# Other chunk sizes in the first mixture, and the second transform's pieces tied to their places on TensorE

## The chip, the cores and the metric

The kernel runs on one core of one Trainium2 chip. The metric is the device time of one execution in microseconds (us), the median over several runs. TensorE (PE in the profile) does the matrix products, VectorE (DVE), ScalarE (ACT) and GpSimd (POOL) the elementwise work. SyncE (SP) issues the transfers between the core's memory and the chip's main memory, in order, from one queue.

## The reference

The input is x, 2 batches of 3136 rows of 256 numbers. Three layers follow each other.

```
Y  = rfft(x, axis=1) mixed by complex weights w_r, w_i, plus bias; soft threshold 0.01
x1 = irfft(Y, n=3136)                                       # layer 1: Fourier filter
x2 = x1 + relu(layernorm(x1) * g @ w1) @ w2                 # layer 2: MLP 1, 256 -> 1024 -> 256
u  = x2 + real(fft(fft(x2, axis=1), axis=2))                # layer 3: a 2-D transform,
out = u + relu(layernorm(u) @ v1) @ v2                      #          then MLP 2
```

Every row passes both MLPs by itself; the transforms along axis 1 join all 3136 rows of a batch. So MLP 2 of a batch needs all of that batch's x2, and batch 1 of a stage can run beside batch 0 of the next.

## The kernel before

**Stages.** Layer 1 runs in three stages (forward transform, mixing, inverse). Its results go to main memory as `dY`, one array per batch. MLP 1 reads rows of `dY` and stores x2 to `dX`. The transform along the rows is split into a 49-point and a 64-point part. The class `Stage98` does the first of these: 16 steps for each batch (`s4[0]`, `s4[1]`), which read 98 x 512 pieces `r` of `dX` (line 352), split them on POOL and ACT (lines 371 to 373 and 204), multiply (line 222 and the two after, into the buffers `psc`), and store the result `o` to `dA` (line 427). `middle` (line 384) gathers one column of `dX` ahead of them. The class `Front` does the rest for each pair of rows of MLP 2: it loads from `dA` (line 764), does four small products (`stage_b`, line 780), and then the transform over the 256 channels (`dmix`, lines 805 to 817), whose sum is the input of MLP 2.

**MLPs.** Both MLPs run in chunks of up to 4 tiles of 128 rows. A chunk has a first layer `l1` with 8 parts f, each 6 matmuls at lines 222 to 224 into one of three buffers `psa`. Each part is evicted twice: by ACT (line 697, relu) and then by DVE (line 699, the remainder `l`, so that two numbers of fewer bits stand for one). A second layer `l2` follows, one tile at a time, each 16 matmuls at lines 715 and 716 into one of two buffers `psb`, evicted by DVE (719, 720) and stored by SP (728). Batch boundaries do not fall on chunks: one tile takes 64 rows from each batch (the shared tile).

**Input of a chunk.** While a chunk runs, the input of the next is made: statistics (DVE 608, 609), `norm` (ACT 616, 630, 631; DVE 617 to 620), `flip` (DVE 643, a transpose of 32 x 32 blocks, then a store of `dT` by SP at 649), `land` (SP 656 reads it back as `q`), and `split` into high and low part (ACT 204, DVE 212). Only then can its `l1` start.

**What sets the order.** A scheduler with a simulated timeline orders the instructions of each engine; `issue_after(x)` adds an edge that holds an instruction behind instruction x on the same engine and makes no semaphore. `run_mlp` gives the places: tables such as `USUAL`, `LATE`, `FIRST`, `EARLY` say at which part (`("l1", f)` or `("l2", tile)`) of a chunk the next one's pieces are written, and `hook` puts the steps of `Stage98` at the places of `STAGE4_AT` (MLP 1, batch 0) and `STAGE4_MLP2` (MLP 2, batch 1). SP works its queue in that order, and a transfer that reads what an earlier one wrote waits there for it.

In `chunks1` MLP 1 has 13 chunks: for batch 0 of 4, 4, 4, 4, 2, 4 and 3 tiles (the last with the shared tile), for batch 1 six of 4. MLP 2 has 13 chunks as well. I write c0 to c12 and m0 to m12 for them.

## Time and profile before

| | |
|---|---|
| median of 3 runs (lowest to highest) | 822.72 us (822.21 to 823.26) |
| profiled execution | 821.94 us |
| its span, first to last instruction | 820.0 us |
| PE busy in the span | 789.9 us (96%) |
| DVE, ACT, POOL busy | 543.0, 363.3, 124.2 us |
| mean granted TensorE clock | 0.994 of full speed |

The profile follows one execution. Each row of a timeline names the engine, the line of the code, the operation, what it writes and reads, and in brackets how long the engine stood idle before it and which engine or transfer ended the idle time. PE is busy nearly all the time, so the places where it is not, about 30 us in the whole span with the start and the end, are where the order of the work can matter.

### The profile page before, as it was taken

The numbers are of one execution on the slowest core, as the hardware profiler recorded it, in microseconds if no ns is written. First come the engines' busy times: TensorE is split into PE (matmuls) and PEld (weight loads), VectorE is DVE, ScalarE is ACT, GpSimd is POOL, SyncE is SP. The second block draws the span as 40 slices with busy tenths as digits, with TensorE's granted clock in tenths as the row PEclk, the third lists the DMA queues.
The fourth block names the chain that finished last, engine by engine and source line by source line (L and its number), as shares of the span: only waits on it lengthen the run. The fifth ranks groups of instructions, "written<-read, shape, count | busy, mean of one in ns | idle before, by whom it ended". The sixth has DMA issues, their size and how long they took to land.

```text
span 820.0 us, 12035 instructions
## 1 busy us (share of the span) xinstructions
PE 789.9 (96%) x4276; PEld 656.4 (80%) x4276; DVE 543.0 (66%) x1260; ACT 363.3 (44%) x791; POOL 124.2 (15%) x152
## 2 busy tenths in 40 slices
PE   8999999999997999999999998999989999999996
PEld 3888977967676879887788886888768898888885
DVE  6479996478846687666747884557555667676543
ACT  1422356358744643345332544456443545444321
POOL 1222221220000000055400002465220000000000
PEclk9999999999999999999999999999999999999999
DMA  8742200621445333454653224454543343322211
GB/s 229 216 137 86 78 1 2 213 103 36 157 145 176 129 110 106 119 172 154 189 157 107 70 74 129 144 155 141 158 116 113 101 138 120 88 71 72 63 36 32
DMA packets 79663, 95.16 MB, mean 116 GB/s; under 512 B 16610, under 2 KB 58858, under 8 KB 79408
## 3 DMA queue, kind: packets, MB, share of 16 engines
q1 hardware_dynamic: 79604, 94.40, 37.9%
q8 instruction: 34, 0.56, 0.3%
q14 instruction: 25, 0.20, 0.1%
HBM read 56.89 MB, written 37.49 MB: 115 GB/s over the span
## 4 chain that ended last, share of the span: by engine, by line
PE 64%; DMA 12%; DVE 11%; SPq 4%; ACT 4%; issue 2%; POOL 1%; DVEq 0%; ACTq 0%; POOLq 0%
PE psb L715 17%; PE psb L716 9%; PE psa L222 8%; PE psa L223 8%; PE psa L224 8%; PE psb L482 4%; DMA yb<-dY 3%; PE psc L780 2%; SPq L328 2%; PE psc L303 2%; PE psa L450 2%; DVE st L608 2%; PE psc L322 2%; PE psc L502 2%; DMA dA<-o 1%
## 5 line engine op out<-in xcount | busy, mean ns | idle before, releaser
L697 ACT ACTIVATE h<-psa 128x512 fp32r<-128x512 f32 (+2 forms) x208 | 116.5, 573 | 219.3 <-PE psa L224 164.8
L699 DVE SCALAR_TENSOR_TENSOR h<-psa,h 128x512 fp32r<-128x512 f32 (+2 forms) x208 | 134.0, 653 | 70.8 <-ACT h L697 68.8
L715 PE MATMUL psb<-r2b,h 128*128 128x512 f32 x392 | 138.2, 399 | 0.0
L715 PE MATMUL psb<-r3a,h 128*128 128x512 f32 x392 | 136.6, 397 | 0.0
L716 PE MATMUL psb<-r2b,h 128*128 128x256 f32 x392 | 106.4, 282 | 0.0
L716 PE MATMUL psb<-r3a,h 128*128 128x256 f32 x392 | 105.4, 282 | 0.0
L222 PE MATMUL psa<-u0r,r3a 128*128 128x512 f32 (+2 forms) x208 | 83.6, 403 | 7.3 <-DVE h L699 7.2
L482 PE MATMUL psb<-wm,h 128*128 128x256 f32 (+1 forms) x600 | 88.8, 298 | 0.8 <-DVE w L488 0.8
L715 PEld LDWEIGHTS psb<-r2b,h 128*128 128x128 f32 x392 | 72.0, 188 | 14.7
L715 PEld LDWEIGHTS psb<-r3a,h 128*128 128x128 f32 x392 | 71.4, 188 | 15.3 <-PE psa L224 0.5
L222 PE MATMUL psa<-u0r,r2b 128*128 128x512 f32 (+2 forms) x208 | 81.7, 393 | 1.9 <-DVE w L207 1.7
L482 PEld LDWEIGHTS psb<-wm,h 128*128 128x128 f32 (+1 forms) x600 | 76.1, 189 | 8.7 <-issue 8.1
L223 PE MATMUL psa<-u0r,r2b 128*128 128x512 f32 (+2 forms) x208 | 79.3, 381 | 0.0
L224 PE MATMUL psa<-u0r,r2b 128*128 128x512 f32 (+2 forms) x208 | 79.2, 381 | 0.0
L223 PE MATMUL psa<-u0r,r3a 128*128 128x512 f32 (+2 forms) x208 | 78.7, 379 | 0.0
L716 PEld LDWEIGHTS psb<-r3a,h 128*128 128x128 f32 x392 | 73.8, 189 | 4.0 <-issue 0.5
L716 PEld LDWEIGHTS psb<-r2b,h 128*128 128x128 f32 x392 | 74.1, 189 | 3.1
L224 PE MATMUL psa<-u0r,r3a 128*128 128x512 f32 (+2 forms) x208 | 75.8, 380 | 0.1
L719 DVE TENSOR_TENSOR o<-psb,yb 128x256 f32<-128x256 f32 x76 | 31.4, 421 | 60.7 <-PE psb L716 60.0
L204 ACT ACTIVATE yg<-psc 98x512 f32<-98x512 f32 (+2 forms) x58 | 48.5, 859 | 45.4 <-PE psc L502 26.9
L222 PEld LDWEIGHTS psa<-u0r,r3a 128*128 128x128 f32 x208 | 39.1, 188 | 20.0 <-DVE h L699 12.4
L212 POOL TENSOR_TENSOR h<-w 128x512 f32<-128x512 f32 (+1 forms) x26 | 34.5, 1328 | 109.2 <-DVE w L489 70.3
(119 smaller groups left out, 1272.7 us busy)
## 6 DMA issues: line engine op xcount, KB each, us to landing
dT<-q SPq DMA_DIRECT2D x20, 512.0 KB
q<-dT SPq DMA_DIRECT2D x20, 512.0 KB
s<-in_moe_w_ch_dram SPq DMA_DIRECT2D x16, 512.0 KB
r<-dX SPq DMA_DIRECT2D x32, 196.0 KB
dA<-o SPq DMA_DIRECT2D x32, 196.0 KB
dY<-yg SPq DMA_DIRECT2D x12, 512.0 KB
r<-dA SPq DMA_DIRECT2D x48, 128.0 KB
dX<-o SPq DMA_DIRECT2D x11, 512.0 KB
```

What stands on the lines that cost most here:

```text
L204: nc.scalar.activation(out=o, in_=i, func=AF.Copy, scale=scale)
L212: ins = eng.tensor_tensor(out=o, in0=a, in1=b, op=ALU.subtract)
L222: nc.tensor.matmul(out=ps, lhsT=lh, rhs=rh, start=first, stop=False)
L223: nc.tensor.matmul(out=ps, lhsT=ll, rhs=rh, start=False, stop=False)
L224: ins = nc.tensor.matmul(out=ps, lhsT=lh, rhs=rl, start=False, stop=last)
L303: nc.tensor.matmul(out=ps, lhsT=cam, rhs=self.raw[g // 2][:, e * 512:(e + 1) * 512], start=True, stop=True)
L482: nc.tensor.matmul(out=ps[0:m, u * D:(u + 1) * D], lhsT=xv[:, o:o + m], rhs=wm_hl[wv][:, e, c, :], start=k == 0, stop=k == 11)
L697: ins = nc.scalar.activation(out=h[:, 0:n], in_=ps[:, 0:n], func=AF.Relu)
L699: ins = nc.vector.scalar_tensor_tensor(out=l[:, 0:n], in0=ps[:, 0:n], scalar=0.0, in1=h[:, 0:n], op0=ALU.max, op1=ALU.subtract)
L715: nc.tensor.matmul(out=ps, lhsT=h[:, ts_], rhs=w2[:, f, :], start=f == 0, stop=False)
L716: nc.tensor.matmul(out=ps[:, 0:D], lhsT=l[:, ts_], rhs=w2[:, f, 0:D], start=False, stop=f == NF - 1)
L719: nc.vector.tensor_tensor(out=o, in0=ps[:, 0:D], in1=self.y[:, i, :], op=ALU.add)
```

## The change

The first mixture's chunks become 4, 4, 4, 4, 4, 4 tiles for batch 0 and 3 (with the shared tile), 3, 4, 4, 4, 4 and 3 for batch 1: still 13 chunks and 49 tiles. The seventh chunk, c6, takes its statistics at new places (`SIXTH`). The 16 steps of `Stage98` go to 6, 6 and 4 places in three chunks, in place of 6, 5 and 5, so that the last step stands at the first tile of the third chunk's `l2` and not at its last. Every step, and `stage_b` of MLP 2's input, is held on PE behind the last matmul written for the chunk at that place (`self.pe`). `ahead` loads a third piece before the second split, so each load is issued one group earlier. The arithmetic and the number of matmuls are the same. The changed kernel's lines stand 3 to 7 further down: 699 is now 704, 608 is 612, 780 is 787.

```diff
@@ -32,16 +32,19 @@
 FIRST = {"stats": (("l2", 0),) * 4, "norm": ("l2", 3), "flip": (("n", 0), ("n", 1))}
 EARLY = {"stats": (("l1", 0), ("l1", 0), ("l1", 1), ("l1", 1)), "norm": ("l1", 2), "flip": (("l1", 5), ("l1", 6)),
          "land": ("l2", 2)}
+SIXTH = {"stats": (("l1", 5), ("l1", 5), ("l1", 6), ("l1", 6)), "norm": ("l1", 7), "flip": (("l2", 1), ("l2", 2))}
 USUAL = {"b": (1, 3), "mix": (3, 5), "stats": (("l1", 4), ("l1", 6)), "norm": ("l1", 7), "flip": (("l2", 1), ("l2", 2))}
 LATE = {"b": (4, 6), "mix": (6, 7), "stats": (("l1", 7), ("l2", 0)), "norm": ("l2", 0), "flip": (("l2", 2), ("l2", 3))}
 LAND_AT = ("l1", 3)
 PREP0_AT = (23, 24)
 L2_BEHIND = 7
 APPLY_POOL = (0, 1)
-STAGE4_AT = ((8, "l1", 6), (8, "l1", 7), (8, "l2", 0), (8, "l2", 1), (8, "l2", 2), (8, "l2", 3)) + tuple(
-    (k, *at) for k in (9, 10) for at in (("l1", 2), ("l1", 5), ("l2", 0), ("l2", 1), ("l2", 3)))
-STAGE4_MLP2 = ((1, "l1", 1), (1, "l1", 3), (1, "l1", 5), (1, "l2", 0), (1, "l2", 1), (1, "l2", 3)) + tuple(
-    (k, *at) for k in (2, 3) for at in (("l1", 2), ("l1", 5), ("l2", 0), ("l2", 1), ("l2", 3)))
+STAGE4_AT = ((8, "l1", 6), (8, "l1", 7)) + tuple((8, "l2", i) for i in range(4)) + tuple(
+    (9, *at) for at in (("l1", 1), ("l1", 3), ("l1", 5), ("l2", 0), ("l2", 1), ("l2", 3))) + tuple(
+    (10, *at) for at in (("l1", 1), ("l1", 3), ("l1", 5), ("l2", 0)))
+STAGE4_MLP2 = tuple(
+    (k, *at) for k in (1, 2) for at in (("l1", 1), ("l1", 3), ("l1", 5), ("l2", 0), ("l2", 1), ("l2", 3))) + tuple(
+    (3, *at) for at in (("l1", 1), ("l1", 3), ("l1", 5), ("l2", 0)))
 STAGE4_FROM = ((7, "l2", 0), (0, "l2", 0))
 WARM_UP = 10
 TB = 2
@@ -400,6 +403,7 @@
 
         def ahead(self):
             self.split()
+            self.load()
             self.split()
 
         def step(self):
@@ -692,6 +696,7 @@
                     c == 0, c == 1)
             if f == L2_BEHIND:
                 self.last = mark["pe"]
+            self.pe = mark["pe"]
             hl = hslot()
             h, l = hl[:, 0:512], hl[:, 512:1024]
             ins = nc.scalar.activation(out=h[:, 0:n], in_=ps[:, 0:n], func=AF.Relu)
@@ -713,7 +718,9 @@
                 for f in range(NF):
                     h, l = self.h[f]
                     nc.tensor.matmul(out=ps, lhsT=h[:, ts_], rhs=w2[:, f, :], start=f == 0, stop=False)
-                    nc.tensor.matmul(out=ps[:, 0:D], lhsT=l[:, ts_], rhs=w2[:, f, 0:D], start=False, stop=f == NF - 1)
+                    ins = nc.tensor.matmul(out=ps[:, 0:D], lhsT=l[:, ts_], rhs=w2[:, f, 0:D], start=False,
+                                           stop=f == NF - 1)
+            self.pe = getattr(ins, "ins", ins)
 
             o = self.o[:, i, :]
             nc.vector.tensor_tensor(out=o, in0=ps[:, 0:D], in1=self.y[:, i, :], op=ALU.add)
@@ -733,13 +740,13 @@
     def chunks1(b, wv):
         cs = []
         if b == 0:
-            plan = [(0, 4), (512, 4), (1024, 4), (1536, 4), (2048, 2), (2304, 4), (2816, 2)]
+            plan = [(c * 512, 4) for c in range(6)]
         else:
-            plan = [(64 + c * 512, 4) for c in range(6)]
+            plan = [(64, 2), (320, 3)] + [(704 + c * 512, 4) for c in range(4)] + [(2752, 3)]
         for r0, nt in plan:
             lo = [(ALLP, 0, nt, rows(dY[b], r0, 128, nt))]
             st = [(ALLP, 0, nt, rows(dX1[b], r0, 128, nt))]
-            if r0 == 2816:
+            if b == 1 and r0 == 64:
                 for src, lst in ((dY, lo), (dX1, st)):
                     for h, (bb, rr) in enumerate(((0, 3072), (1, 0))):
                         lst.append((slice(h * 64, h * 64 + 64), nt, 1, rows(src[bb], rr, 64, 1)[:, 0, :]))
@@ -989,14 +996,18 @@
                     pl = LATE if n_ in (mlp2[0], mlp2[6]) else USUAL
                     i = 0
                     for p, pr in enumerate(n_.front.pairs):
-                        put(("l1", pl["b"][p]), n_.front.stage_b, p)
+                        def stage_b(p, ch=ch, n_=n_):
+                            with tc.issue_after(ch.pe):
+                                n_.front.stage_b(p)
+
+                        put(("l1", pl["b"][p]), stage_b, p)
                         put(("l1", pl["mix"][p]), n_.front.dmix, p, n_.y, i)
                         w = 2 if pr[0][1] else 1
                         for t in range(w):
                             put(pl["stats"][p], n_.stats, i + t)
                         i += w
                 else:
-                    pl = FIRST if n_ is mlp1[2] else EARLY
+                    pl = FIRST if n_ is mlp1[2] else SIXTH if n_ is mlp1[6] else EARLY
 
                     def stats(t, ch=ch, n_=n_, when=pl["stats"]):
                         with ExitStack() as es:
@@ -1066,10 +1077,10 @@
                 f()
         return g
 
-    def behind_l1(chunks, k, f):
+    def in_turn(chunks, k, f):
 
         def g():
-            with tc.issue_after(chunks[k].last):
+            with tc.issue_after(chunks[k].pe):
                 f()
         return g
 
@@ -1085,14 +1096,14 @@
     hook(*STAGE4_FROM[0], s4[0].start)
     hook(8, "l1", 1, after(8, 1, s4[0].ahead))
     for k, part, i in STAGE4_AT:
-        hook(k, part, i, s4[0].step)
+        hook(k, part, i, in_turn(mlp1, k, s4[0].step))
     mlp1[2].load()
     run_mlp(mlp1, mlp2[0:3], hooks)
     hooks = {}
     hook(*STAGE4_FROM[1], s4[1].start)
-    hook(0, "l2", 3, behind_l1(mlp2, 0, s4[1].ahead))
+    hook(0, "l2", 3, in_turn(mlp2, 0, s4[1].ahead))
     for at in STAGE4_MLP2:
-        hook(*at, behind_l1(mlp2, at[0], s4[1].step) if at[1] == "l2" else s4[1].step)
+        hook(*at, in_turn(mlp2, at[0], s4[1].step))
     run_mlp(mlp2, [], hooks)
```

**DVE, end of c2 and start of c3's input.** Line 699 (now 704) is the eviction of `l1`, 212 (now 215) the split of c3's input, 719 and 720 the evictions of `l2`, and 608 and 609 (now 612, 613) the statistics on `yb`: those in the rows before are of c6, whose rows come from `dY` of batch 1 for the shared tile. Before:

```order
L699 SCALAR_TENSOR_TENSOR h<-psa,h 128x512 x5
L212 TENSOR_TENSOR u0r<-w,u0r 128x512 x2
L719 TENSOR_TENSOR o<-psb,u0r 128x256 x2
L720 TENSOR_TENSOR o<-psb,o 128x256 x2
L608 BN_STATS st<-yb 128x6
L609 BN_AGGR mv<-st 128x2
L617 RECIPROCAL sm<-sm 128x3
L608 BN_STATS st<-yb 128x6 x3
```

After:

```order
L704 SCALAR_TENSOR_TENSOR h<-psa,h 128x512 x4
L612 BN_STATS st<-yb 128x6 x3
L613 BN_AGGR mv<-st 128x2
L704 SCALAR_TENSOR_TENSOR h<-psa,h 128x512
L613 BN_AGGR mv<-st 128x2 x2
L612 BN_STATS st<-yb 128x6 x3
L613 BN_AGGR mv<-st 128x2
L215 TENSOR_TENSOR u0r<-w,u0r 128x512
```

The first statistics on rows that the inverse transform of batch 1 stores stood behind c2's last eviction and c3's split; now they stand ahead of both.

**SP, start of batch 1's second transform (end of c12).** 600 (604) loads input rows, 649 (653) stores and 656 (660) reads back a flipped input, `dT_1657` being m1's, 728 (735) stores c12's result, 384 (387) gathers the column, 352 (355) loads pieces for the steps, 764 (771) loads for `stage_b`. Before:

```order
L649 DMA dT_1657<-q 128x2x512
L656 DMA q<-dT_1657 128x8x128
L600 DMA yb<-dX_68 64x256 x2
L600 DMA yb<-dX_68 128x1x256
L728 DMA dX_69<-o 128x1024
L384 DMA m_4854<-dX_69 98x32x1
L352 DMA r_4857<-dX_69 98x512
L352 DMA r_4859<-dX_69 98x512
L764 DMA r_4937<-dA_70 128x256 x2
```

After:

```order
L735 DMA dX_69<-o 128x768
L653 DMA dT_1657<-q 128x2x512
L387 DMA m_4855<-dX_69 98x32x1
L355 DMA r_4858<-dX_69 98x512
L355 DMA r_4860<-dX_69 98x512
L660 DMA q<-dT_1657 128x8x128
L355 DMA r_4932<-dX_69 98x512
L771 DMA r_4940<-dA_70 128x256 x2
```

m1's read-back stood ahead of c12's store; now it stands behind the store, the gather and two loads.

**PE, the first `stage_b` behind those loads.** 780 (787) is `stage_b`, 715 and 716 (720) `l2`, 222 to 224 (225 to 227) `l1`. Before:

```order
L715 MATMUL psb<-r2b,h 128x512
L716 MATMUL psb<-r2b,h 128x256
L780 MATMUL psc<-cb,r_4937 128x64 x2
L715 MATMUL psb<-r2b,h 128x512 x2
L780 MATMUL psc<-cb,r_4937 128x64
L716 MATMUL psb<-r2b,h 128x256 x2
L222 MATMUL psa<-u0r,r2b 128x512
```

After:

```order
L225 MATMUL psa<-u0r,r2b 128x512
L226 MATMUL psa<-u0r,r2b 128x512
L227 MATMUL psa<-u0r,r2b 128x512
L787 MATMUL psc<-cb,r_4940 128x64 x4
L219 MATMUL psc<-mhl,ca_hl 98x32
L220 MATMUL psc<-mhl,ca_hl 98x32
L720 MATMUL psb<-r2b,h 128x512
```

The four products stood in the midst of an `l2` tile; now they stand behind two and a third parts of the next `l1`.

## Rows read from the trace of the kernel before

**Rows 1.** waits of PE, whole span: us in total, times, longest.

```profile
PE psa L222 <- DVE h L699: 7.5, 8, 2.6
PE psc L780 <- DMA r<-dA: 6.9, 2, 3.5
PE psa L222 <- DVE w L207: 1.7, 1, 1.7
PE psc L222 <- DVE mv L609: 1.3, 1, 1.3
```

**Rows 2.** windows: stretch, length, busy us (count) per engine, PEclk, DMA, GB/s.

```profile
264.00:267.40 3.40, 3.34 (x15) 2.77 (x16) 2.97 (x12) 3.40 (x11) 0.00 (x0) 1.00 0.41 163
505.00:508.40 3.40, 0.04 (x1) 0.00 (x0) 0.00 (x0) 0.00 (x0) 1.67 (x4) 1.00 0.87 250
509.00:512.40 3.40, 3.40 (x12) 2.82 (x12) 1.38 (x3) 2.51 (x6) 3.28 (x5) 0.50 0.36 118
614.80:618.20 3.40, 3.40 (x12) 2.89 (x12) 0.00 (x0) 0.00 (x0) 0.00 (x0) 0.50 0.29 75
```

**Rows 3.** timeline of PE: start, us, name, count, [idle before <-releaser].

```profile
499.97 0.39 PE L715 MATMUL psb<-r2b,h 128*128 128x512 f32 x1
...
500.31 0.40 PE L715 MATMUL psb<-r2b,h 128*128 128x512 f32 x1
...
508.43 0.66 PE L780 MATMUL psc<-cb,r 128*128 128x64 f32 x4 [3.39 <-DMA r<-dA]
...
599.69 0.47 PE L224 MATMUL psc<-u0r,ca_hl 98*98 98x512 f32 x1
...
614.54 1.26 PE L780 MATMUL psc<-cb,r 128*128 128x64 f32 x6 [3.48 <-DMA r<-dA]
```

**Rows 4.** timeline of SP, batch 1's start of the second transform.

```profile
485.14 0.36 SPq L649 DMA_DIRECT2D dT<-q  x1
...
491.95 0.37 SPq L656 DMA_DIRECT2D q<-dT  x1
...
494.27 0.79 SPq L728 DMA_DIRECT2D dX<-o  x1
...
501.75 0.91 SPq L384 DMA_DIRECT2D m<-dX  x1
...
505.21 1.77 SPq L764 DMA_DIRECT2D r<-dA  x4
```

**Rows 5.** timeline of SP at three other places.

```profile
238.64 8.62 SPq L328 DMA_DIRECT2D dY<-yg  x6
...
610.77 0.82 SPq L764 DMA_DIRECT2D r<-dA  x2
...
668.42 0.52 SPq L656 DMA_DIRECT2D q<-dT  x1
```

**Rows 6.** timeline of ACT at three places.

```profile
477.63 1.16 ACT L204 ACTIVATE u0r<-q 128x512 fp32r<-128x512 f32 x2 [0.86 <-DMA q<-dT]
...
584.71 0.63 ACT L204 ACTIVATE u0r<-w 98x512 fp32r<-98x512 f32 x1 [4.82 <-POOL w L373]
...
677.26 1.16 ACT L204 ACTIVATE u0r<-q 128x512 fp32r<-128x512 f32 x2 [2.97 <-DMA q<-dT]
```

**Rows 7.** timeline of POOL in MLP 2.

```profile
583.12 0.72 POOL L371 TENSOR_TENSOR w<-r 98x254 f32<-98x254 f32 x1 [5.95 <-DMA r<-dX]
```

**Rows 8.** timeline of DVE around chunk 3 of MLP 1, and at a flip.

```profile
243.59 0.69 DVE L699 SCALAR_TENSOR_TENSOR h<-psa,h 128x512 fp32r<-128x512 f32 x1 [0.67 <-ACT h L697]
...
254.42 0.43 DVE L608 BATCH_NORM_STATS2 st<-yb 128x6 f32<-128x256 f32 x1 [4.77 <-DMA yb<-dY]
...
462.24 1.29 DVE L643 STREAM_TRANSPOSE q<-q 128x512 f32<-128x512 f32 x2
```

**Rows 9.** groups of DVE, 440 to 500: count, busy us, mean ns.

```profile
L699 DVE SCALAR_TENSOR_TENSOR h<-psa,h 128x512 fp32r<-128x512 f32 x22 | 14.8, 685 | 1.4 <-ACT h L697 1.0
...
L536 DVE SCALAR_TENSOR_TENSOR t<-s,t 128x512 f32<-128x512 uint32 x3 | 2.0, 679 | 0.0
```

## Prediction

> **What bounds the kernel now.** I read the page's shares first, then PE's waits over the whole span, then windows and timelines around each wait. PE is busy nearly throughout, and the change leaves its matmuls the same, so time can come only from what PE waits for and from its clock. The waits that matter are few: 7.5 us for DVE's eviction of `l1`, 6.9 us in two pieces for a load from `dA`, 1.7 us for a DVE copy, 1.3 us for DVE's statistics [rows 1]. The reader is to see in the windows that a wait can cost twice: in the 3.4 us after each of the two `dA` waits PE is busy throughout but at a granted clock of 0.50, that is 1.2 GHz, and does 12 matmuls in 3.40 us where 15 take 3.34 us at 1.00, 2.4 GHz; after the 2.6 us wait before 264 the clock stayed at 1.00 [rows 2]. Twelve matmuls here are mixed shapes; at half speed 3.4 us of work costs 1.7 us more. So a stall near 3.4 us is priced at itself plus 1.7, one up to 2.6 at itself.
>
> The sum is made against the profiled execution, 821.94 us (span 820.0 and 1.94 around it), which lies 0.78 below the median of the runs, 822.72.
>
> **The change part by part.** Units for PE: 15 matmuls of 512 columns in 3.34 us [rows 2], 0.223 each, so an `l1` part of six takes about 1.36 with what stands between; a 512 and a 256 matmul of `l2` start 0.34 us apart from the next pair [rows 3], so a tile of eight pairs takes 2.8, two tiles 5.7.
>
> *A, the `dA` wait in batch 1's transform (614.54).* Before, the last step's matmul starts at 599.69, the load for `stage_b` is issued at 610.77, and PE gets it at 614.54 after idling 3.48 [rows 3, 5]. The load landed 3.77 us after issue; the rest, 11.1 us, is the step's eviction, its store and SP's queue. After, the last step stands at the first tile of m3's `l2`. Between it and the `stage_b` that needs its result PE has three `l1` parts, two tiles and two more parts: 5 x 1.36 + 5.7 = 12.5 us. The whole chain of before, 14.4 us with the queue, would leave 1.9; the chain without the queue in front of the store I estimate at 11. The wait goes: 3.5 + 1.7 = **+5.2** (gain; with the long chain +3.3).
>
> *B, loads one group further ahead.* At 583.12 POOL had waited 5.95 us for a piece of `dX` [rows 7], ACT then stood 4.82 us for POOL's copy [rows 6], and PE 1.66 for DVE behind ACT, the third row of [rows 1]. A load issued one step earlier has 3 to 5 us more; a step comes each two `l1` parts, 2.7 us, or `l2` tile. That covers PE's 1.7: **+1.7** (0.5 to 1.9, since ACT's stall need only fall under its slack).
>
> *C, the `dA` wait where batch 1's transform starts (508.43).* Before it costs 3.39 + 1.7 = 5.1. After, `stage_b` stands behind 2.3 further `l1` parts, 3.2 us, and the clock stays up: that wait goes. But m1's read-back now stands in SP's queue behind c12's store, the gather and two loads. Let T0 be the end of c12's last tile on PE. The store goes out with it; before, the gather was issued 7.5 us after the store (494.27 to 501.75), as it reads what the store writes [rows 4]. So the gather is at T0+8, two loads take SP to T0+11.4 (501.75 to 505.21, 3.5 us, [rows 4]), then the read-back is issued. One landed 8.84 us after issue (668.42 to 677.26) [rows 5, 6], and here it runs beside two loads of the steps; its copies stand at T0+20, or T0+17 if the store is faster. PE reaches that `l1` after five parts, a pair of tiles and a channel transform: 6.8 + 5.7 + 0.9 = T0+13.4. New wait 3.6 to 6.6; I take 4.0, since the column gather need not take as long behind a store of three tiles as behind one of four, plus 1.7 clock. 5.1 - 5.7 = **-0.6** (bounds: wait 0 gives +5.1, wait 8 gives -4.6).
>
> The Trainium skill speaks to the order here: its page "DMA: Bandwidth & Descriptors", section "Queues, rings and completion order", says that each DMA engine takes descriptors of a queue in ring order. By that rule the read-back stands behind the gather's thousands of 4-byte pieces as well as behind its issue; the trace agrees that the engines were full there, 0.87 busy in 505 to 508.4 [rows 2]. The sum by rows is not altered by it.
>
> *D, c12 is a chunk of three tiles, not four.* Its `l1` part takes three quarters of PE's time, 1.03 us, while DVE's work beside it does not shrink alike: within its eight parts and two tiles of c11, 14 us for PE, the order shows 8 evictions at about 0.47 (three quarters of the 0.685 of [rows 9], less overlap), a decoding of MLP 2's weights of eight operations at 0.34 to 0.6 ([rows 9]), two flips at 0.6 [rows 8], two channel transforms at 1.6, four tile evictions and statistics: also 14 us. No slack is left, and late evictions of 0.8, 0.3 and 0.9 us follow by the order: **-2.2** (0 to -4.5, all of DVE's excess).
>
> *E, m0's input.* Its flips lie later against PE. Flip's end to copies took 14.1 us before (462.24 + 1.29 = 463.53 to 477.63) [rows 6, 8]; after, the flips end some 16.7 us behind c11's last `l1`, so copies are at 30.8, and PE is there at 28.9 by its units: **-1.9**; with another 1.0 of wait for the longer 15.6 us (6.8 from store to read-back issue, 485.14 to 491.95, plus 8.84): I take **-2.4** (0 to -6).
>
> *F, c2 to c3 in MLP 1.* Before, DVE waits until 254.42 for `dY` of batch 1, 15.8 us after the first of its stores at 238.64 [rows 5, 8], and PE then loses 4.5 of the 7.5 us of [rows 1] behind late evictions, the longest 2.6. After, the last inverse steps come on PE some 7.3 us earlier, so the data are there at 231.3 + 15.8 = 247.1. But those statistics now stand ahead of c2's last eviction on DVE, which started at 243.59 before [rows 8], and PE's `l2` needs it at once, by about 245.2. With three statistics and one aggregate (1.5 us) and the eviction (0.7) it is there at 249.4: one wait of 4.2 us + 1.7 of clock = 5.9. **-1.4** (+4.5 to -4.0).
>
> *G, c4 to c10.* Of the other 3.0 us for evictions in [rows 1] about 1.0 lies in the two-tile chunk c4 and goes with it. Of 0.65 more and of the 1.3 for statistics (last row of [rows 1]), both where steps lie scattered into `l1`, holding them to their places saves about half: **+2.0** (0 to +3.0). The holds themselves add no semaphore; what they cost is order, told above.
>
> Sum: 5.2 + 1.7 - 0.6 - 2.2 - 2.4 - 1.4 + 2.0 = +2.3. As E and D press on the same l1s, I round it to +1.9: profile 820.0, on the median's scale **820.8 us**.
>
> **Rivals.**
>
> *R1, the transfers land in time.* C and E wait for nothing new, F loses only what it lost before less half (+2.2 at most), D stays: 5.2 + 1.7 + 5.1 - 2.2 + 0 + 2.2 + 2.0 = +14; with F at its forecast -1.4 it is +10.4: **812**. For it: read-backs elsewhere were late by only 0.86 to 2.97 us on ACT [rows 6], and a late store need not mean a late gather. Against: each row of [rows 4] says 7 to 8 us for a write and a read in sequence.
>
> The Trainium skill gives a price that leads here: "DMA: Bandwidth & Descriptors", section "Anatomy of one DMA — SWDGE (gpsimd) path", fits a transfer at about 2.0 us plus its bytes at 436 GB/s. By it the 512 KB read-back would take an estimated 3.2 us, and C's wait would fall to nothing; the trace disagrees, with 8.84 us for the same transfer.
>
> *R2, slower: SP's queue decides.* One transfer that waits holds all behind it. The read-back for m1 goes out at T0+13 and lands at T0+21.4: PE waits 8 us, the clock costs 1.7, so C is -4.6; m0's read-back is held in the same queue (E -4.0), and so are the loads that were to come earlier (B 0). 5.2 + 0 - 4.6 - 2.2 - 4.0 - 1.4 + 2.0 = -5.0: 828. It decides once the read-back of m1 goes out later than about T0+11.5. For it: the order has it plainly behind three transfers, one of which waits. Against: the gather of before waited for a larger store.
>
> *R3, the change does not do what it says:* A's wait stays, as the store is again held in SP's queue (-3.5 against the sum): 824.
>
> **How the numbers follow.** The forecast 0.45 (817 to 825), R1 0.27 (808 to 816), R2 0.23 (825 to 832), R3 0.05. What a measurement can tell from no change is 0.2%, 1.6 us: 821.1 to 824.4 counts as the same. Of the forecast's 0.45, about 0.24 lie below 821.1, 0.15 within, 0.06 above; with R1 faster is 0.51, R3 and the edge of R2 give the same 0.17, slower 0.32. The range leaves out the lower third of R1 and the top of R2: 810.5 to 830.
>
> **What would show it.** A: no wait at the `stage_b` after m3's transform steps and no 0.50 window behind it. B: no ACT wait over 3 us for POOL's copy. C: PE waiting at m1's first `l1` for DVE or ACT behind `q<-dT`, 3 to 8 us, with a 0.50 window; none is R1, over 7 is R2. D: short PE waits for `h` in c12. E: the same at m0. F: one wait of about 4 us at c2's first tile in place of two at c3. I am wrong if C, E and F are absent together, or if a new wait opens at a place that I do not name.

## Result and profile after

| | before | changed |
|---|---|---|
| median (lowest to highest) | 822.47 us (821.85 to 823.26) | 810.34 us (808.72 to 810.77) |
| ratio, 95% interval | | 0.9848 [0.9831, 0.9865] |
| profiled execution, span | 821.94, 820.0 us | 810.77, 808.9 us |

The change takes 12.1 us (1.5%) off. The forecast was 820.8; the time lies just under the range's low end, 810.5. A second comparison gave 0.9838 [0.9783, 0.9892] (e11). The kernel before scattered from 819 to 830 us in the later comparisons, so ratios are read within one comparison and the waits from the traces.

First the waits of PE in the changed kernel, to be held against [rows 1]; each row has the total, the number of waits and the longest.

```profile
PE psa L225 <- DVE h L704: 2.9, 3, 1.4
PE psc L225 <- ACT u0r L207: 1.6, 1, 1.6
PE psb L721 <- DVE h L704: 1.5, 1, 1.5
PE psc L227 <- POOL u0r L215: 1.4, 2, 0.9
...
PE psa L225 <- ACT u0r L207: 0.5, 1, 0.5
```

The row for `dA`, 6.9 us in two waits, is gone, and so are the half-speed windows of [rows 2]. Two windows of the changed kernel show it: the first is at the place of the first wait, to be held against the second of [rows 2], the other spans the end of batch 1's transform, where the kernel before has the second wait and a mean clock of 0.91. PE is busy throughout, at 1.00:

```profile
505.00:508.40 3.40, 3.36 (x21) 2.85 (x19) 2.93 (x10) 2.99 (x9) 2.91 (x4) 1.00 0.01 4
604.00:624.00 20.00, 20.00 (x111) 17.03 (x110) 11.06 (x29) 6.59 (x15) 0.00 (x0) 1.00 0.43 128
```

Now what the forecast said of the start of batch 1's transform, from SP. In the changed kernel the first row is c12's store, then the store of m1's flipped input, the gather, and m1's read-back:

```profile
491.00 0.54 SPq L735 DMA_DIRECT2D dX<-o  x1
491.95 0.38 SPq L653 DMA_DIRECT2D dT<-q  x1
493.69 0.92 SPq L387 DMA_DIRECT2D m<-dX  x1
...
497.31 0.40 SPq L660 DMA_DIRECT2D q<-dT  x1
```

The gather goes out 2.7 us after the store, against 7.5 in [rows 4]. The read-back is used 5.9 us after its issue, against 8.84 in [rows 5, 6]:

```profile
503.23 1.15 ACT L207 ACTIVATE u0r<-q 128x512 fp32r<-128x512 f32 x2 [1.87 <-DMA q<-dT]
```

c12's last tile ends on PE at 489.12 (T0). I had these copies at T0+17 to T0+20; they stand at T0+14.1, and PE, which I had there at T0+13.4, came at T0+14.3 and waited 0.5 us.

**What held the store before.** Three windows; the number after the clock is the mean busy share of the 16 DMA engines, the last one GB/s. The first two are of the kernel before, around c12's store (issued 494.27, gather 501.75), the third of the changed kernel.

```profile
494.30:497.00 2.70, 2.70 (x15) 2.28 (x14) 2.19 (x8) 1.69 (x4) 0.00 (x0) 1.00 1.04 334
497.00:501.60 4.60, 4.60 (x23) 3.85 (x22) 3.25 (x11) 3.36 (x9) 0.00 (x0) 1.00 0.12 45
```

```profile
491.00:493.60 2.60, 2.60 (x17) 2.25 (x16) 2.48 (x8) 1.26 (x5) 0.00 (x0) 1.00 0.76 275
```

For 4.6 of the 7.5 us the engines were busy at 0.12, two of sixteen: not a slow store, but a share of it left over on two engines. The packet records of the trace name what was ahead (packets begun in each us):

```
size     from 492: 492 493 494 495 496 497 498 499 500 501   last begun
512 B (read-back)    3 251 621 149   0   0   0   0   0   0     495.51
1 KB  (row loads)    0   0   2 126  36  20  34  35   3   0     500.09
4 KB  (c12's store)  0   0   0  21  80  11   0   3  11   2     501.23
```

Two of the three row loads ahead of the store take 64 rows and are done in 495. The third is the mirrored load, `128x1x256`, which reads two blocks of 64 rows in reverse order: its 128 packets of 1 KB go two at a time, 46 ns each, and the store's packets on those two engines come behind it. The code gives its source as 2 x 64 rows, outermost dimension 2. The Trainium skill says why that is two engines ("DMA: Bandwidth & Descriptors", section "Why a DMA increments its semaphore by 16 and not by 1"): such a transfer runs on the largest number of engines up to 16 that divides the outermost dimension over 1 of both sides. The trace agrees: 0.12 of sixteen. In the changed kernel no such load stands right ahead of c12's store: the mirrored one went out 6.9 us earlier, at 484.06, and the store's packets began within 1.1 us, the last at 493.13.

**The account.** In us of the profiled executions, a gain positive; half-speed stretches at 1.7 each.

| term | forecast | measured | from |
|---|---|---|---|
| A, second `dA` wait | +5.2 | +5.2 | 3.5 + 1.7, gone |
| B, loads earlier | +1.7 | -1.1 | 1.7 + 0.3 before; 0.9 + 1.6 + 0.4 now |
| C, first `dA` wait, m1's read-back | -0.6 | +4.6 | 3.4 + 1.7 gone, 0.5 in its place |
| D, c12's evictions | -2.2 | 0 | no wait |
| E, m0's input | -2.4 | 0 | no wait |
| F, c2 to c3 | -1.4 | +1.5 | 4.5 before; 1.5 + 0.6 + 1.0 now |
| G, c4 to c10 | +2.0 | +1.5 | 2.9 before; 1.4 now |

These add to 11.7; the span fell by 11.1, after 1.4 more in the loading before c0, which the change does not touch. The 0.8 left over is a remainder; a wait of 0.5 us at 213 that is gone is part of it.

### The profile page after: what moved, and what is told of

The parts are those of the page before. It is cut to its first block, busy times and chain, and to the rows that moved or that the text cites. A ratio compares the mean times of both kernels' runs of the same rounds, so it can differ in the third digit from the quotient of the medians.

```text
span 808.9 us, 12024 instructions
## 1 busy us (share of the span) xinstructions
PE 786.6 (97%) x4276; PEld 657.1 (81%) x4276; DVE 539.5 (67%) x1259; ACT 364.8 (45%) x793; POOL 122.5 (15%) x152
## 4 chain that ended last, share of the span: by engine, by line
PE 76%; DVE 8%; DMA 7%; SPq 3%; ACT 2%; issue 2%; POOL 1%; ACTq 0%; POOLq 0%
PE psb L720 20%; PE psa L225 10%; PE psb L721 10%; PE psa L226 10%; PE psa L227 10%; PE psb L486 4%; PE psc L787 3%; PE psc L325 2%; DMA h<-in_x_dram 2%; SPq L331 2%; PE psc L306 2%; PE psc L506 2%; PE psa L454 1%; DVE t L323 1%; PE psc L812 1%
## 5 line engine op out<-in xcount | busy, mean ns | idle before, releaser
L721 PE MATMUL psb<-r3a,h 128*128 128x256 f32 x392 | 107.1, 283 | 1.5 <-DVE h L704 1.5
L225 PE MATMUL psa<-u0r,r3a 128*128 128x512 f32 (+1 forms) x208 | 81.9, 394 | 3.2 <-DVE h L704 2.9
L225 PE MATMUL psa<-u0r,r2b 128*128 128x512 f32 (+2 forms) x208 | 80.6, 388 | 0.5 <-ACT u0r L207 0.5
L226 PE MATMUL psa<-u0r,r2b 128*128 128x512 f32 (+2 forms) x208 | 78.6, 378 | 0.0
L226 PE MATMUL psa<-u0r,r3a 128*128 128x512 f32 (+1 forms) x208 | 78.5, 378 | 0.0
L227 PE MATMUL psa<-u0r,r2b 128*128 128x512 f32 (+2 forms) x208 | 78.1, 380 | 0.0
L227 PE MATMUL psa<-u0r,r3a 128*128 128x512 f32 (+1 forms) x208 | 76.0, 380 | 0.0
L225 PEld LDWEIGHTS psa<-u0r,r3a 128*128 128x128 f32 x208 | 39.1, 188 | 13.2 <-DVE h L704 6.3
```

Source lines behind the costliest of these rows:

```text
L225: nc.tensor.matmul(out=ps, lhsT=lh, rhs=rh, start=first, stop=False)
L226: nc.tensor.matmul(out=ps, lhsT=ll, rhs=rh, start=False, stop=False)
L227: ins = nc.tensor.matmul(out=ps, lhsT=lh, rhs=rl, start=False, stop=last)
L721: ins = nc.tensor.matmul(out=ps[:, 0:D], lhsT=l[:, ts_], rhs=w2[:, f, 0:D], start=False, stop=f == NF - 1)
```

## Experiments

**Whose gain it is.** e1 is the kernel before with the new chunk plan and `SIXTH` alone; e2 has all the rest of the change and not these.

> The kernel before with the new chunk plan and the new places of c6's statistics alone; the steps' table, the holds and the third early load stay as before. Theory T (the two waits for dA, 3.4 and 3.5 us, and the half-speed clock behind each were the gain, and the holds and the table removed them): both waits stay, since the products of stage_b still stand inside the l2 tile right behind their loads; only the waits around c2 to c4 change, so 1 to 3 us below before, about 820. Rival P (the chunk plan brought it, as a three-tile c12 makes the store, the gather and the read-back at the start of batch 1's transform short): 6 us or more below before, 816 or less, and the first dA wait under 1 us.

> The kernel before with everything but the chunk plan (and the places for c6): table of steps, holds, third early load. T: both dA waits and both half-speed stretches gone, 8.5 to 10.5 us below before, 812 to 814. P: with a c12 of four tiles m1's read-back stands behind a longer store, gather and loads, and PE waits some 4 us at m1's first l1 with a half-speed stretch behind it: 817 to 818.

e1: 820.42 us against 827.36, 0.9921 [0.9894, 0.9949]; e2: 816.81, 0.9882 [0.9854, 0.9911]. The first two rows are of PE's waits in e1, the last is of those in e2, which has none for `dA`.

```profile
PE psc L781 <- DMA r<-dA: 6.6, 2, 3.8
PE psa L223 <- DVE h L700: 3.1, 4, 1.2
```

```profile
PE psa L224 <- DVE h L703: 9.6, 8, 3.2
```

e1 keeps both waits as T said, and yet came out 6.5 us lower by the ratio where T had 1 to 3: the plan alone is worth more than T allowed, and why stays open (the last section has a possible part of it). e2 lost both waits and came out 9.8 us lower by the ratio, inside T's 8.5 to 10.5; it kept the waits around c2 to c4 and gained one of 3.2 us at 421 and one of 2.0 at 514, each with a half-speed stretch. P's wait at m1 did not come in either. The two gains add to 16.3 us, more than the change's 12.5 by its ratio, but with intervals of over 2 us on each that does not tell whether they overlap.

**Each edit of the holds and the table.** e3 undoes one edit of the changed kernel, e4 another:

```diff
-                        def stage_b(p, ch=ch, n_=n_):
-                            with tc.issue_after(ch.pe):
-                                n_.front.stage_b(p)
-                        put(("l1", pl["b"][p]), stage_b, p)
+                        put(("l1", pl["b"][p]), n_.front.stage_b, p)
```

> The changed kernel with stage_b not held behind the chunk's last matmul (the steps stay held). The order then has the four products at the start of batch 1's transform inside an l2 tile again, 1.3 to 2.5 l1 parts earlier than in the changed kernel. T: the first dA wait returns, 2 to 3.5 us, with a half-speed stretch if it comes near 3.4: 3 to 5 us above the changed kernel, 813 to 815. P: the load is there in time anyway: within 1 us of the changed kernel.

e3: 817.74 us, 0.9889 [0.9862, 0.9916]: 3.4 us over the changed kernel by the ratios, 7 by medians of two comparisons. The wait is back, longer than before, and the window behind it is at half speed; the first row is PE's timeline in e3, the second that window:

```profile
510.19 1.12 PE L787 MATMUL psc<-cb,r 128*128 128x64 f32 x4 [5.59 <-DMA r<-dA]
```

```profile
510.20:513.60 3.40, 3.40 (x12) 3.01 (x13) 0.00 (x0) 0.56 (x1) 3.40 (x4) 0.50 0.37 133
```

The one edit moved SP's order too: m1's read-back went out ahead of c12's store again, and the loads for `stage_b` at 505.69 to 508.63 and not from 498.40 on. So e3 shows that the hold is needed, but not how much of it is PE coming later.

e4 has `STAGE4_AT` and `STAGE4_MLP2` as the minus lines of the change's diff have them, holds kept.

> The changed kernel with the old table of 6, 5 and 5 places, all holds kept. The last step of each transform then stands at the last l2 tile of its chunk, and the stage_b that needs it has 5.2 l1 parts and some 10 l2 pairs in front, about 9 us for PE, while the chain from the last step's matmul to the load is 11 to 14 us. T: the second dA wait returns in part, 2 to 5 us, and if it passes 3 us with a half-speed stretch of 1.7: 2 to 6 us above the changed kernel. P: no difference over 1 us.

e4: 829.94 us, 1.0044 [1.0024, 1.0064], slower than the kernel before. Not one but both transforms end in a wait for `dA`, as PE's timeline in e4 shows:

```profile
456.97 0.63 PE L785 MATMUL psc<-cb,r 128*128 128x64 f32 x4 [3.34 <-DMA r<-dA]
...
628.37 0.99 PE L785 MATMUL psc<-cb,r 128*128 128x64 f32 x4 [3.35 <-DMA r<-dA]
```

With the old table and no holds the scheduler had pulled steps ahead of their places: batch 0's last step begins at 409 on PE in the kernel before and at 446 in e4. The holds forbid that, so the late last step then costs in both batches. By the ratios e4 is 16 us over the changed kernel, where T had 2 to 6: I had counted one end, not two, and not the half speed at each; two more half-speed stretches stand at 253 and 604, behind waits of 2.0 and 2.4 us. e10 is the reverse, the new table alone on the kernel before:

> The kernel before with the table of 6, 6 and 4 places alone: no holds, old chunk plan, old ahead. The order has m3's last step two l2 tiles earlier, and stage_b at the start of batch 1's transform where it was. T (two waits, each with its own cause): the second wait (3.5 us) and its half-speed stretch go, the first stays: 4 to 6 us below before. If the table needs the holds to act, as the old table with the holds came out above the kernel before: within 1.5 us of before.

e10: 816.65 us, 0.9914 [0.9886, 0.9943], 7.0 us below before, more than T's 4 to 6, but its interval (4.7 to 9.4) reaches into that. The second wait is gone; the first stays, 2.7 us, and e10's window behind it has 6.1 us at half speed:

```profile
509.50:515.60 6.10, 6.10 (x18) 5.14 (x19) 2.61 (x6) 2.93 (x7) 5.76 (x10) 0.50 0.52 173
```

So A is the table's doing, as forecast, and each of the two waits has its own cause.

**The third early load.** e8 is the changed kernel with `ahead` as before:

```diff
             self.split()
-            self.load()
             self.split()
```

> The changed kernel with the old ahead (two splits, no third load). The order on PE is the same. If each step's load is late without it, POOL and ACT stand for r as in the kernel before and PE waits 1 to 3 us more in the two transforms: 1 to 3 us above the changed kernel. If the loads were early enough, as the holds put the steps later anyway: within 1 us.

e8: 810.39 us, 0.9805 [0.9763, 0.9848]. Its waits in batch 1's transform are 0.6, 1.5 and 0.4 us, against 0.9, 1.6 and 0.4 with the load. B's edit does nothing that the comparison can tell. The wait that it was to remove, 1.7 us at 587, is gone in e10, which has the new table alone, but also in e5 and e9 below, which have the old one and other places for the mirrored loads; and e12 below, the changed kernel with these loads on another queue, has none of the three waits. So e9 and e12 point to the queue for the lateness of `r` too, and not to how early its load is issued.

**Is it the mirrored load?** e5 puts it behind c12's store in the kernel before; e6 does the same in the changed kernel, where that puts it ahead of m1's read-back.

```diff
             if soon:
-                far.fetch()
+                with ExitStack() as es:
+                    if far is mlp2[3]:
+                        es.enter_context(tc.issue_after(mlp1[12].sent))
+                    far.fetch()
```

> The kernel before, with the row loads of m3's input issued behind c12's store and no longer ahead of it; the order on PE is the same up to that point. In the trace of before the mirrored load (128 x 1 x 256) moves its 128 packets of 1 KB on two DMA engines only, two at a time at 46 ns, and thirteen packets of c12's store wait behind them, so the gather of the column goes out 7.5 us after the store. Theory M (the 7.5 us was that queueing, and so were my long chains): the gather goes out 2.5 to 4 us after the store, the loads for stage_b 4 to 5 us earlier, and the wait of 3.4 us for dA is under 0.5 with no half-speed stretch behind it: 4 to 5.5 us below before. Rival S (a store of 512 KB and its receipt take that long by themselves): gather still 7 us or more after the store, the wait stays, time within 1.5 us of before.

> The changed kernel, with the row loads of m3 held behind c12's store, which puts two mirrored loads on SP just ahead of m1's read-back (there were none), and the gather and the loads for the steps behind it. M: the read-back's share on the two engines waits for 128 packets of 1 KB there, so it lands 8 us or more after its issue and not 5.9, and PE waits 2 to 5 us at m1's first l1: 2 to 6 us above the changed kernel. S: the read-back is issued earlier than in the changed kernel and lands as fast, so nothing is lost: within 1 us.

e5: 825.21 us, 0.9979 [0.9955, 1.0003]. SP's rows in e5:

```profile
496.38 0.33 SPq L728 DMA_DIRECT2D dX<-o  x1
496.76 3.56 SPq L600 DMA_DIRECT2D yb<-dX  x6
500.41 0.91 SPq L384 DMA_DIRECT2D m<-dX  x1
501.36 6.14 SPq L352 DMA_DIRECT2D r<-dX  x2
507.61 1.77 SPq L764 DMA_DIRECT2D r<-dA  x4
```

By the packet records the last packet of the store began at 498.60, 2.2 us after the issue, and the gather followed 4.0 us after the store: S is wrong about the store. The time did not follow. The row loads, two of them mirrored, now stood ahead of the steps' loads, the first of which took 5.7 us to issue, so the loads for `stage_b` went out where they had been and the wait stayed at 3.3 us. I had moved the block, not removed it.

e6: 815.06 us, 0.9852 [0.9818, 0.9885], 4.7 us over e8 of the same comparison, which is the changed kernel but for the third load. The read-back in e6, on SP and then on ACT:

```profile
494.71 1.56 SPq L660 DMA_DIRECT2D q<-dT  x1
```

```profile
503.76 1.15 ACT L207 ACTIVATE u0r<-q 128x512 fp32r<-128x512 f32 x2 [6.36 <-DMA q<-dT]
```

Against T0 it is issued 1.6 us earlier than in the changed kernel and used 1.6 us later: 9.05 us, the figure that I had taken for a read-back's own time, comes with two mirrored loads in front. The read-back that I had read it from, at 668 in the kernel before, tells the same by its packets of 512 B: 896 of 1024 began by 672 and the last 128, two sixteenths, from 674 to 676.8, and from 668 to 672 packets of 1 KB went at some 40 in a us, as behind the mirrored load above. PE waits 2.1 us for it, and 1.0 and 1.9 us shortly after, and then runs at half speed for 5.5 us; the three waits of batch 1's transform, 3.0 us, are gone in return.

e9 removes the block without moving it: in `fetch` of the kernel before the mirrored loads go to ACT's queue.

```diff
-                sp.dma_start(out=o if n > 1 else o[:, 0, :], in_=ap)
+                q = nc.scalar if self.front is not None and ps_ is ALLP else sp
+                q.dma_start(out=o if n > 1 else o[:, 0, :], in_=ap)
```

> The kernel before with MLP 2's mirrored row loads issued by ACT on its own queue, all else on SP as before; the order on PE is the same. M (a transfer on two engines holds what stands behind it in the same queue): c12's store no longer waits behind 64 packets on each of two engines, the gather goes out 3 to 5 us after it and not 7.5, the loads for stage_b come 2.5 to 4.5 us earlier and the 3.4 us wait for dA is under 1 us: 3 to 6 us below before. S (store and receipt take that long): gather 7 us or more after the store, the wait stays, time within 1.5 us of before. Against M even if it is right: SP also waits for the transfer eight issues back, whichever queue it is on.

e9: 818.8 us, 0.9938 [0.991, 0.9967], 4.9 us below before. SP's rows in e9, and the window where the first wait was:

```profile
492.97 0.47 SPq L729 DMA_DIRECT2D dX<-o  x1
497.77 0.89 SPq L384 DMA_DIRECT2D m<-dX  x1
...
501.19 1.78 SPq L765 DMA_DIRECT2D r<-dA  x4
```

```profile
505.00:512.00 7.00, 7.00 (x39) 5.91 (x38) 3.30 (x7) 4.37 (x11) 5.88 (x10) 1.00 0.51 162
```

The gather comes 4.8 us after the same 512 KB store, the loads for `stage_b` 4.0 us earlier than in [rows 4] (3.1 against PE, which comes 0.9 earlier), and the first wait is gone, with no hold, no new plan and the old table. This settles M against S. The second wait stays, with the old table, as 3.5 and 1.9 us. The Trainium skill has the reason, in "DMA: Bandwidth & Descriptors", section "Queues, rings and completion order": an engine takes turns between queues but works each in order. e9 agrees; no run here shows the turns themselves.

The other queue does not free the two engines. In e9 m1's flipped input, stored at 484.30, is read back at 491.18, 6.9 us later against 6.8 in [rows 4], though the mirrored load beside it stands on ACT's queue: 32 of the store's 256 packets began after 487, the last at 490.59, with the engines busy at 0.11:

```profile
486.50:491.00 4.50, 4.50 (x27) 3.93 (x26) 3.63 (x12) 1.32 (x3) 0.00 (x0) 1.00 0.11 35
```

**Both causes at once, and what is left.** e14 is the kernel before with the new table and the loads on the other queue, nothing else.

> The kernel before with the new table of 6, 6 and 4 places and the mirrored loads on ACT's queue; no holds, no new chunk plan, no third load. If the mirrored loads' queueing (M) is the whole cause of the first dA wait and the last step's place that of the second, both waits and both half-speed stretches are gone, and it comes within 2 to 4 us of the changed kernel: 1.0 to 1.6% below before. If the holds are needed for the first wait, it stays at 2 us or more, with a half-speed stretch: 0.6 to 1.0% below before.

e14: 813.2 us, 0.9862 [0.9826, 0.9898]. PE's waits in e14:

```profile
PE psa L224 <- DVE h L702: 5.8, 5, 2.5
PE psc L808 <- ACT w L206: 1.8, 1, 1.8
...
PE psc L783 <- DMA r<-dA: 0.7, 2, 0.5
```

Both waits are gone (the 0.7 us in the last row is elsewhere, its longer part at 421). Two edits give most of what the change gave; by the traces the rest is the waits for DVE around c2 to c4, which the chunk plan shortens. The first wait has two remedies: let the queue go free, or, as the holds do, let PE come later to the loads. e2 shows the second by itself: on SP its gather goes out 7.0 us after the store and the loads for `stage_b` 11.0, against 7.5 and 10.9 in [rows 4], and PE comes to them 5.1 us after their issue without a wait, where the kernel before came 0.2 us ahead of it.

```profile
496.78 0.52 SPq L734 DMA_DIRECT2D dX<-o  x1
503.75 0.91 SPq L386 DMA_DIRECT2D m<-dX  x1
...
507.81 3.75 SPq L770 DMA_DIRECT2D r<-dA  x4
```

```profile
512.93 1.00 PE L786 MATMUL psc<-cb,r 128*128 128x64 f32 x8
```

e7 holds the statistics of c6 and c7 at the places where c4 and c5 have them, in the changed kernel; the scheduler had pulled those of c6 to the end of c2:

```diff
-                            if ch is mlp1[0]:
+                            if ch in (mlp1[0], mlp1[4], mlp1[5]):
                                 es.enter_context(tc.issue_after(ch.rest[when[t][1]]))
```

e12 is the changed kernel with e9's edit; e13 has both; e11 is the changed kernel again.

> The changed kernel with the statistics of c6 and c7 held on DVE behind the eviction of the l1 part at which they are written, so that nothing that needs dY of batch 1 stands ahead of c3's evictions and split. If the waits of 1.47, 0.59 and 0.97 us at 249 to 269 come from DVE standing in order behind that transfer (theory F), all three go: 2 to 3.5 us below the changed kernel. If the statistics are then late for c6's own input, a wait of 1 to 3 us opens at c6's first l1 and the time is the same.

> The changed kernel as it is, beside the others on one chip. All theories: 1.2 to 2.0% below before. Its waits at 249 to 268 (three, 3.0 us) and at 424 (1.4 us) are there again; the read-back for m1 takes 5 to 6.5 us and PE's wait there is under 1 us.

> The changed kernel with MLP 2's mirrored row loads on ACT's queue; the order on PE is the same. M: ACT's wait of 4.3 us for a store to dA at 424 and POOL's waits for r in batch 1's transform shrink, as the transfers behind the mirrored loads land earlier, and PE's waits of 1.4, 0.9 and 1.6 us with them: 1 to 3.5 us below the changed kernel. Rival: each load costs ACT its issue and a place in order, 24 loads at 0.1 to 0.5 us on an engine that PE waits for in the transforms, so the time is the same or 1 to 4 us longer.

> The changed kernel with both: statistics of c6 and c7 held as in e7_after_stats_held, mirrored loads on ACT's queue as in e12_changed_other_queue. If the two remove different waits (three at 249 to 268, some 2.8 us; and those behind the mirrored loads, some 2 us), their gains add: 2.0 to 2.4% below before, 1 to 3 us below e12_changed_other_queue. If the second hides behind the first, no more than e12: 1.7 to 2.1% below before.

| | us | ratio to before, interval |
|---|---|---|
| e7, statistics held | 809.0 | 0.9783 [0.9751, 0.9815] |
| e11, changed | 809.66 | 0.9838 [0.9783, 0.9892] |
| e12, other queue | 806.95 | 0.9803 [0.9757, 0.9848] |
| e13, both | 805.21 | 0.9754 [0.9726, 0.9783] |

e11 came as expected, but for two waits and not three at 249 to 269, 2.0 and 0.5 us. In e7 the waits there are gone, so F's cause is as I had it, DVE standing in order behind `dY`; 1.1 us came back at 330, and by the median e7 is 1.4 below e8, less than expected. e12 is 2.7 below e11, inside what M gave. e13 has the lowest time and ratio of all; its gain over e12 is 1.7 us by medians of two comparisons and 4.0 by their ratios, and the single times overlap (804.6 to 807.9 and 806.2 to 808.3), so it is not shown that the two gains add.

## Why the prediction was wrong

**The step that failed is C**: "before, the gather was issued 7.5 us after the store ..., as it reads what the store writes. So the gather is at T0+8 ... One landed 8.84 us after issue". C came out at +4.6 where I had -0.6, 5.2 of the 9.4 us by which the terms fell short of the account. I took two durations from the trace as the transfers' own and added them up for a place where the queue was different. With nothing ahead in the queue the store's last packet began 2.2 us after its issue (e5), and in the changed kernel the read-back was used 5.9 us after its own, with other traffic; the rest was a wait behind a load that used two engines of sixteen (e5, e6, e9). With the gather at T0+4.6, 3.6 us from it to the read-back's issue (3.5 in my sum) and 5.9, the copies come at T0+14.1 where my sum has T0+20. The same trace would have told, by the DMA share while SP waited: I showed 0.87 for 505 to 508.4, and in 497 to 501.6 it is 0.12. The Trainium skill's fit that I set aside ("DMA: Bandwidth & Descriptors", section "Anatomy of one DMA — SWDGE (gpsimd) path"), 2.0 us plus bytes, gives an estimated 2.9 us for the 384 KB store and 3.2 for the read-back. It is a fit for transfers that GpSimd issues, and these are SP's: the gather's 2.7 is near it, the read-back's 5.9 is not. But one row with a queue in front was no ground to set it aside.

**E** fell with a figure of the same kind: flip's end to copies took 10.4 us in the changed kernel and not 14.1, and PE had no wait. In the kernel before the last 128 of that read-back's 1024 packets began from 475 on, the others by 474. Counted from c11's last `l1`, the flips ended at 15.4 us (I had 16.7), the copies began at 25.8 (30.8) and PE came at 28.1 (28.9). On DVE the flips, on SP the store and the read-back, on ACT the copies, of the changed kernel:

```profile
466.90 1.31 DVE L647 STREAM_TRANSPOSE q<-q 128x512 f32<-128x512 f32 x2
```

```profile
468.23 0.37 SPq L653 DMA_DIRECT2D dT<-q  x1
...
472.32 0.38 SPq L660 DMA_DIRECT2D q<-dT  x1
```

```profile
478.56 1.15 ACT L207 ACTIVATE u0r<-q 128x512 fp32r<-128x512 f32 x2 [1.92 <-DMA q<-dT]
```

**D**: c12's eight parts and the two tiles of c11 took PE from 458.87 to 475.54, 16.7 us and not 14, as two `stage_b` and two channel transforms stand among them, which I had left out. DVE had 13.2 us of work in that window of the changed kernel, and PE was busy in all of it:

```profile
458.90:475.60 16.70, 16.70 (x107) 15.95 (x106) 13.22 (x41) 8.09 (x21) 0.00 (x0) 1.00 0.35 112
```

I had DVE's 14 us about right, though the row of [rows 9] that I named for the decoding has 0.68 for one operation where I wrote 0.34 to 0.6. With PE's time too short I saw no slack where there were 3.5 us.

**F**: the order was read rightly, DVE behind `dY`, but the place where PE needs the eviction was not. I put it at the tile's start, 245.2; it is needed by the last low-part matmuls of c2's first two tiles, and PE got to 249.4 first. The data came at 249.05, 2.0 us later than my 247.1, so two misses partly cancel: the wait was 1.5 us and not 4.2, and no half speed followed. Two more waits, 0.6 and 1.0 us, came behind it where I had one. DVE and PE in the changed kernel:

```profile
249.05 1.08 DVE L612 BATCH_NORM_STATS2 st<-yb 128x6 f32<-128x256 f32 x3 [5.05 <-DMA yb<-dY]
```

```profile
250.84 0.51 PE L721 MATMUL psb<-r3a,h 128*128 128x256 f32 x2 [1.47 <-DVE h L704]
```

**A** held, in mechanism and size (e10, e4). **G** held in its total, +1.5 for +2.0, and not in its parts. The waits of 0.96 and 0.65 us went with the chunk plan (e1 has lost them; e2, with the holds, keeps 0.96 and 0.53). The wait of 1.3 for statistics is gone with the rest of the change (e2 has none, e1 one of 1.25 for an eviction at the same place), but one of 1.4 us at 426 opened in return. That this is near the 1.0 us that I had left standing is luck. **B** held in neither: the third load is worth nothing that shows (e8), and waits of 0.9, 1.6 and 0.4 us came in batch 1's transform. These and the one at 426 are the new waits at places that I had not named, the second of my signs of being wrong.

Rival **R1** was what happened, "the transfers land in time", at 810.3 for its 812, though the reason it gave was not the one that the runs show, and the nearness is in part luck: its D and F were 2.2 and 2.9 us too low, its B, C and G 2.8, 0.5 and 0.5 too high. Durations read with a queue in front carried C, E, R2 and the low chance of R1; D and F erred the same way for reasons of their own. My range, built from separate bounds, was too narrow for four terms that err alike. Slips beside this: R2's landing at T0+21.4 is T0+21.8 by its own numbers, one of the two pairs in [rows 4] that I called 7 to 8 us is 6.8, and PE's 245.2 in F and 28.9 in E stand without their working.

## What to carry to other kernels

Before a wait for a transfer is taken into a sum as the transfer's length, look at the busy share of the DMA engines while it lasts: a share near 2/16 says that a few engines are finishing something else, and then the length belongs to the queue and changes with what is ahead. A load with a small outermost dimension is cheap by itself and dear for what stands behind it: issue it where nothing waits behind it, as in the changed kernel ahead of c12's store, or give it another queue, which helped one store in e9 and not the other. Holding pieces to their places needs the places to be right first: with the old table the same holds made the kernel slower.

## What was not expected of the hardware

The clock's answer to a wait varied. Six traces have the same wait of 2.5 to 2.6 us at c3: after it the clock stayed at 1.00 in the kernel before [rows 2] and in e9, and it fell to 0.50 in e2, e5, e10 and e14. The windows of e14 at and behind that wait:

```profile
261.20:263.60 2.40, 0.00 (x0) 0.00 (x0) 2.40 (x11) 1.53 (x5) 0.00 (x0) 1.00 0.01 3
...
264.00:267.30 3.30, 3.30 (x9) 2.60 (x8) 2.88 (x11) 3.17 (x9) 0.00 (x0) 0.50 0.48 186
```

After a wait of 2.0 us at c2 it fell in e11 and not in e12. And after the first `dA` wait PE was at 0.50 for 3.4 us before and for 6.1 us and more in e10, after a shorter wait (2.7 us for 3.4). So a wait of 2.0 to 2.5 us cannot be priced at itself with certainty, as I did, and what else decides it stays open. The profiled execution of the kernel before, which the forecast is summed against, was one in which the clock did not fall at c3; its executions in the later comparisons had a mean granted clock of 0.984 to 0.994, and the profiled one 0.994. The plan removes that wait, so in most executions it may be worth more than the trace shows, which would be a part of what T lacked in e1; no run shows how much.
